# Block-recurrent cross attention with a maxout layer: state and A transposes moved from TensorE to DMA, a new prologue order, state reads in pairs

## The chip, the cores and the metric

The kernel runs on one core of one Trainium2 chip. The metric is the device time of one launch in microseconds (us). TensorE (PE) does the matmuls and the transposes through an identity matrix; VectorE (DVE) and ScalarE (ACT) move results out of the accumulation banks in PSUM and do elementwise work; GpSimd (POOL) does casts and products in SBUF; SyncE (SP) issues nearly all DMAs, in the order of the program. Each engine takes its own instructions in order and waits for the others by semaphores, so an instruction that waits holds up all behind it on its engine.

## What is computed

```python
B, H, S, Ns, D = 8, 8, 512, 32, 64
scale = 1 / sqrt(D)
a     = softmax(scale * x @ state^T)        # per batch and head, 512 x 32
xread = a @ state                           # 512 x 64
a2    = softmax(scale * state @ x^T)        # 32 x 512
sread = a2 @ x                              # 32 x 64
t     = concat([xread, sread], rows)        # 544 rows per batch; heads side by side: 4352 x 512
out   = max(t @ w1, t @ w2) @ w_out         # w1, w2: 512 x 1024, w_out: 1024 x 512
```

## The kernel before

**The algebra.** The maximum is rewritten: max(h1, h2) = h2 + relu(h1 - h2). With wd = w1 - w2 and wwo = w2 @ w_out, out = t @ wwo + relu(t @ wd) @ w_out. For the x rows, t is itself a product A @ state (A: the normalised weights), so the kernel first multiplies the states with the weights (SW = state x [wd, wwo], `sw_mm`, L301) and then A with SW. Per batch b: `xt` (x transposed), `sc` (scores, L214) and their exponential e on ACT, `red` (row sums and reciprocals, DVE), `nm` (the product a = e / sum, L240), `at` (a transposed into aT), `sw`, then `l1` (L334: r = relu(aT x SW), eight tiles f) and `l2` (L362: four output tiles c, each of two matmuls with aT and eight with r). `sr` (L270 to L293) is the second read: e^T x, scaled by its reciprocal sums (`sr_ev`, L280), transposed and put into sread_t, from which the last 256 output rows are made at the end (`m1`, `m2`).

**The states.** sbd (L105) holds, per batch and pair of heads, the transposed states of the two heads in block-diagonal form: for a pair k, partitions 0 to 63 carry head 2k in columns 0 to 31, and partitions 64 to 127 carry head 2k+1 in columns 32 to 63; the rest is zero. Before, sbd is set to zero as a whole (L440), `cS` (L160) casts the states to bf16 with each head written twice side by side (sb), `S` (L165) transposes 128x128 blocks on TensorE, and two evictions `S.lo.hi.j` (L173) copy only the diagonal parts. Steps S.0.1 and S.1.2 serve batches 0 and 1, S.2.4 and S.4.8 the batches 2 to 7. `sc` and `sw` read sbd.

**Transposes by DMA.** `xtd` (L200) makes xt of a batch from a bf16 copy of x (xb, written by `cb`), and `atd` (L256) makes aT from a. Batches 2 to 7 have both by DMA. Batches 0 and 1 have x and A transposed on TensorE (`xt`, `at`) and evicted by DVE or ACT.

**What sets the order.** The prologue, all work up to `sc`, `nm` and `atd` of batch 2, is one list written out, ORDER (L18 to L41), run token by token by `step` (L508). A token with `:` and bank numbers is TensorE work into those PSUM banks; a token with `>A`, `>V` or `>P` is work of ACT, DVE or POOL; a token with neither is a DMA, all on SP. The numbers are batch and part: `sw.0.3:1,4` is the fourth quarter of SW of batch 0 into banks 1 and 4, `sw.0.3.0>A` its first eviction by ACT, and `swh.1.0` is half a row of SW of batch 1. `ww.i.f0.f1` is part of wwo, `sub.q` part of wd = w1 - w2, `cw2` and `w2` cast, transpose and evict w2, `cwo` casts w_out. `l2p.0.c.f0.f1` is part of output tile c of batch 0, `l2o` its two matmuls with aT; `ld...` are loads. `idle.n.w` is n matmuls of w columns on a zero tile, which compute nothing. The order within each engine is the order of the list, so a bank that is not evicted yet or an eviction that stands behind a waiting one stops what follows.

Behind the list stands a loop over b = 1 to 6 (L526). An iteration issues the transposes for later batches, does `l1` of batch b, `sc`, `nm` and `atd` of batch n = b + 1, output tiles 0 and 1 of b, `sw` of n, the state reads of the batches in `rd` (L555) into one bank of ring "a" (two banks), then output tiles 2 and 3 of b and the store. Before, rd is (2, 0) and (3, 1) in the first two iterations and one batch in each of the other four.

Of the kernel before, what the change touches and what calls it, by code (L numbers as in the profile page):

```python
# [703 lines left out]
```

## Time and profile before

| | |
|---|---|
| three runs | 150.48, 151.10, 151.94 us; median 151.1 |
| the profiled execution | 151.55 us, its span 149.6 us |
| HBM read, written | 15.20 MB, 8.91 MB |
| granted TensorE clock | 1.00 |

The span is the part of the execution that the profile covers. A row of the timeline gives start (us from the span's start), length, engine, source line, operation, written tile <- read tiles, shape, count, and in brackets the idle time ahead of it with what ended it. A row of grouped instructions gives count, busy time and mean ns. In a windows row stand the stretch and its length, then busy time (and count) of PE, PEld (TensorE's weight loads), DVE, ACT and POOL, then the granted clock, the DMA share and GB/s. A DMA row gives count, size and time from issue to landing. "PEq" and "SPq" mean the engine's queue of issuing instructions. Matmuls are pipelined, so the distance between starts, not the length of a row, is what one costs.

### The profile page before, as it was taken

To read this page: it belongs to the slowest core of one execution; us is meant where nothing else is said; L and a number is where in the kernel's file an instruction comes from. 1 tells how busy PE (TensorE), PEld (TensorE's weight loads), DVE (VectorE), ACT (ScalarE), POOL (GpSimd) and SP (SyncE) were. 2 spreads that over 40 slices of the span, in tenths; PEclk is the share of its full clock that TensorE was granted. 3 is DMA by queue.
4 is the path that set the end of the run, shared out by engine and by line. 5 is a ranking of instruction groups with operands and counts; after the bars stand their busy time and mean duration, and the time that the engine had idled before them with its cause. 6 is when DMAs were issued, how large, how long until landed. Compare 5 with 4: busy or idle time off the path is not lost. (4 is left out here: it accounts for less than half of the span.)

```text
span 149.6 us, 3181 instructions
## 1 busy us (share of the span) xinstructions
PE 141.8 (95%) x1281; PEld 71.0 (47%) x1281; DVE 85.0 (57%) x167; ACT 65.9 (44%) x129; POOL 50.7 (34%) x71
## 2 busy tenths in 40 slices
PE   6979779999999999999999999999999999999991
PEld 2656334635445445444544454444445444763460
DVE  3599387976534917662848385558627575720320
ACT  5234544665594438163814554173528054520200
POOL 3123223389300960770582159045600500000000
PEclk9999999999999999999999999999999999999999
DMA  4999999953936199898879767997406031500423
GB/s 115 291 365 364 363 349 361 345 119 42 252 134 278 30 119 286 345 179 251 346 142 205 266 214 145 182 363 163 86 1 280 2 74 70 212 9 9 185 96 140
DMA packets 36692, 29.09 MB, mean 194 GB/s; under 512 B 21568, under 2 KB 34112, under 8 KB 35776
## 3 DMA queue, kind: packets, MB, share of 16 engines
q1 hardware_dynamic: 36400, 28.77, 67.4%
q8 instruction: 11, 0.18, 0.5%
q10 hardware_dynamic: 272, 0.07, 0.2%
q14 instruction: 9, 0.07, 0.2%
HBM read 15.20 MB, written 8.91 MB: 161 GB/s over the span
## 5 line engine op out<-in xcount | busy, mean ns | idle before, releaser
L354 PE MATMUL bank<-wo,r 128*128 128x512 bf16 (+1 forms) x264 | 62.0, 373 | 0.1
L354 PEld LDWEIGHTS <-r 128*128 128x128 bf16 x264 | 25.4, 98 | 29.3 <-issue 1.3
L95 ACT COPY h<-bank 128x512 f32<-128x512 f32 (+1 forms) x17 | 9.5, 574 | 48.0 <-PE bank L354 44.4
L339 PE MATMUL bank<-aT,sw 128*128 128x512 bf16 x128 | 30.1, 379 | 0.0
L330 DVE TENSOR_SCALAR r<-bank 128x512 bf16<-128x512 f32 x28 | 19.4, 692 | 17.5 <-PE bank L339 16.9
L328 ACT ACTIVATE r<-bank 128x512 bf16<-128x512 f32 x36 | 21.3, 612 | 7.3 <-PE bank L339 7.0
L97 DVE CAST sw<-bank 128x512 bf16<-128x512 f32 (+1 forms) x25 | 15.1, 653 | 11.5 <-PE bank L309 11.5
L241 POOL TENSOR_TENSOR a<-e,er 128x512 bf16<-128x512 bf16 x13 | 13.4, 1048 | 23.6 <-ACT e L233 13.7
L99 POOL CAST xb<-h 128x1024 bf16<-128x1024 f32 x12 | 12.2, 1039 | 22.4 <-issue 15.4
L349 PE MATMUL bank<-sw,aT 128*128 128x512 bf16 (+1 forms) x66 | 18.9, 373 | 0.2 <-ACT sr L287 0.2
L339 PEld LDWEIGHTS <-sw 128*128 128x128 bf16 x128 | 12.0, 98 | 12.9
L99 POOL CAST xe<-h 128x512 bf16<-128x512 f32 x27 | 15.8, 621 | 5.9 <-DMA h<-in_x_dram 5.2
L97 DVE COPY h<-bank 128x512 f32<-128x512 f32 (+1 forms) x16 | 10.5, 659 | 11.9 <-PE bank L354 9.9
L95 ACT CAST sw<-bank 128x512 bf16<-128x512 f32 (+1 forms) x27 | 13.2, 559 | 7.6 <-PE bank L309 7.6
L237 DVE TENSOR_REDUCE sums<-e 128x16 f32<-128x512 bf16 x16 | 10.6, 662 | 1.1 <-ACT e L233 1.0
L233 ACT ACTIVATE e<-bank 128x512 bf16<-128x512 f32 x16 | 8.9, 595 | 4.6 <-PE bank L225 4.1
L433 PE MATMUL bank<-wz 128*128 128x256 bf16 (+1 forms) x38 | 7.7, 349 | 1.2 <-DVE ones L438 1.2
L426 PE MATMUL bank<-wo,w2t 128*128 128x512 bf16 x32 | 8.1, 380 | 0.6 <-DVE w2t L97 0.6
L349 PEld LDWEIGHTS <-aT 128*128 128x128 bf16 x66 | 5.5, 98 | 4.8 <-issue 0.7
L309 PE MATMUL bank<-wd,sbd 64*32 64x512 bf16 (+1 forms) x144 | 5.9, 358 | 1.1 <-DVE wd L418 1.1
L99 POOL CAST wo<-h 128x1024 bf16<-128x1024 f32 x3 | 3.1, 1039 | 8.7 <-DMA h<-in_moe_w_out_dram 8.7
L225 PEld LDWEIGHTS <-xt 128*128 128x128 bf16 x128 | 5.0, 98 | 2.1 <-ACT xt L95 0.3
(71 smaller groups left out, 112.1 us busy)
## 6 DMA issues: line engine op xcount, KB each, us to landing
out_dram<-h SPq DMA_DIRECT2D x7, 1024.0 KB, 4.0
h<-in_moe_w_dram SPq DMA_DIRECT2D x8, 512.0 KB, 9.9
h<-in_x_dram SPq DMA_DIRECT2D x8, 512.0 KB, 7.3
h<-in_x_dram SPq DMA_DIRECT2D x3, 1024.0 KB, 6.5
h<-in_moe_w_out_dram SPq DMA_DIRECT2D x4, 512.0 KB, 9.3
h<-in_x_dram SPq DMA_DIRECT2D x4, 256.0 KB, 3.9
out_dram<-h SPq DMA_DIRECT2D x3, 256.0 KB, 2.4
out_dram<-rs SPq DMA_DIRECT2D x2, 256.0 KB, 2.4
```

Of the source, the lines that this page charges most:

```text
L95: nc.scalar.copy(o, i)
L97: nc.vector.tensor_copy(o, i)
L99: nc.gpsimd.tensor_copy(o, i)
L233: nc.scalar.activation(out=e_view(b, hh).rearrange("p (g c) i n -> p g c (i n)", g=2), in_=p.rearrange("p (c g m) -> p g c m", c=NC, g=2), ...
L237: nc.vector.tensor_reduce(es_all[:, b, hh], e_view(b, hh), axis=AXX, op=ALU.add)
L241: (nc.gpsimd if eng == "P" else nc.vector).tensor_mul(e_view(b, hh, "a"), e_view(b, hh), d_(b)["er"][:, hh].unsqueeze(3).to_broadcast([128 ...
L328: nc.scalar.activation(out=o, in_=p, func=ACTF.Relu)
L330: nc.vector.tensor_scalar(o, p, scalar1=0.0, scalar2=None, op0=ALU.max)
L339: nc.tensor.matmul(p, SW[b][:, g, f * 128:(f + 1) * 128], AT[b][:, g].rearrange("p c t -> p (c t)"), start=(g == 0), stop=(g == 1))
L349: nc.tensor.matmul(p[:, lo:hi], AT[b][:, g, c, :], SW[b][:, g, FF + lo:FF + hi], start=(start and g == 0), stop=(stop and g == 1))
L354: nc.tensor.matmul(p[:, lo:hi], R[b][:, f, c * 128:(c + 1) * 128], wo[:, f, lo:hi], start=(start and j == 0), stop=(stop and j == len(fs) ...
L426: nc.tensor.matmul(p, w2t[:, f, i, :], wo[:, f, :], start=(f == 0), stop=(f == NF - 1))
```

## The change

- The states of batches 2 to 7 no longer pass TensorE. A new step `cSm` (`s_mask`) on ACT multiplies the f32 states by one of two columns of a new constant tile zm (1 for the heads of one parity, 0 for the others), so that the zeros of the block-diagonal form stand in sb already. A new DMA, `std` (`s_dma`), transposes all twelve blocks from sb straight into sbd. Steps S.2.4, S.4.8, their evictions and cS.2.8 on POOL go. sbd is set to zero for batches 0 and 1 alone.
- A of batch 1 is transposed by DMA (`atd.1`); at.1.0, at.1.1 and their evictions go.
- On SP the order becomes: the states of batches 2 to 7 (ldS.2.8) ahead of x of batch 2, then atd.1, xtd.2, std, x of batch 3.
- ORDER is new as a whole: other engines for many evictions and casts, other banks, another order on TensorE, 44 instead of 34 fillers of 256 columns (and the same four of 512).
- State reads come as (0, 1), (2, 3), (4, 5), (6, 7) in iterations 1, 2, 4 and 6; iterations 3 and 5 have none.

```diff
--- before.py
+++ after.py
@@ -17,27 +17,26 @@
 
 ORDER = """
 ldS.0.1 ldxk.0.0 ldxk.0.1 ldxk.0.2 ldxk.0.3 ldw2.0.256 ldwo.0.2 ldw1.0.256 ldw2.256.512 ldwo.2.4 ldw1.256.512
-ldw2.512.768 ldwo.4.6 ldw1.512.768 ldx.1.0 ldx.1.1 ldw2.768.1024 ldwo.6.8 ldw1.768.1024 ldx.2.0 ldx.2.1 ldS.2.8
-idle.4.512:7 cS.0.1>A S.0.1:0 idle.7.256:2 S.0.1.0>V S.0.1.1>A ce.0.0>P cS.1.2>V xt.0.0:6 ce.0.1>V S.1.2:2
-S.1.2.0>A xt.0.0>V xt.0.1:3 idle.3.256:5 S.1.2.1>V xt.0.1>A ce.0.2>V ce.0.3>V xt.0.2:4 sc.0.0:5 xt.0.2>V xt.0.3:1
-sc.0.0>A idle.5.256:0 xt.0.3>V cw2.0>P red.0.0>V sc.0.1:7 idle.6.256:6 sc.0.1>A nm.0.0>V w2.0:0 cwo.0>A
-idle.8.256:2 w2.0>V red.0.1>V ww.3.0.2:6 sub.0.2.4>P ww.1.0.2:2 ww.0.0.2:3 ww.2.0.2:4 nm.0.1>V idle.5.256:1 cw2.1>A
-sub.0.0.2>V at.0.0:5 at.0.1:1 w2.1:7 at.0.0>V at.0.1>A cwo.1>P w2.1>V sw.0.0:0,5 sw.0.0.0>A sw.0.0.1>A ww.1.2.4:2
-sub.1.0.2>V l1.0.0:1 ww.2.2.4:4 sub.1.2.4>V l1.0.0>A ww.0.2.4:3 cw2.2>V sw.0.1:0,7 swh.1.0:5,1 sw.0.1.1>A
-ww.3.2.4:6 sw.0.1.0>V swh.1.0.0>A w2.2:7 swh.1.0.1>V l1.0.3:0 cwo.2>P w2.2>V l1.0.1:5 l1.0.3>A l1.0.2:1 l1.0.1>A
-ww.2.4.6:4 sub.2.0.2>V ww.3.4.6:6 l1.0.2>A ww.0.4.6:3 sub.2.2.4>V l2p.0.2.0.2:7 ce.1.0>V sw.0.2:0,5 l2p.0.2.2.4:7
-sw.0.2.1>A sw.0.2.0>V ce.1.1>P xt.1.0:1 l1.0.5:5 xt.1.0>V xt.1.1:0 ce.1.2>P l1.0.5>A l1.0.4:1 xt.1.1>V ww.1.4.6:2
-ce.1.3>A l1.0.4>V sc.1.0:5 l2p.0.0.0.2:0 sc.1.0>A cw2.3>V xt.1.3:1 l2p.0.2.4.6:7 xt.1.3>A red.1.0>V w2.3:5 xt.1.2:1
-l2p.0.0.2.4:0 cwo.3>P w2.3>V xt.1.2>A l2p.0.0.4.6:0 sc.1.1:1 nm.1.0>V ww.2.6.8:4 sc.1.1>A ww.1.6.8:2 sub.3.2.4>V
-ww.2>A ww.3.6.8:6 ww.0.6.8:3 red.1.1>V sub.3.0.2>P ww.1>A l2p.0.1.0.2:5 ww.3>A l2p.0.1.2.4:5 ww.0>V l2p.0.1.4.6:5
-nm.1.1>P sw.0.3:1,4 swh.1.2:2,6 sw.0.3.0>A sw.0.3.1>V l2p.0.3.0.2:3 cb.2.1>P swh.1.2.1>A swh.1.2.0>V at.1.0:1
-l1.0.6:4 at.1.0>A at.1.1:6 cb.2.0>P l1.0.7:2 l1.0.6>A at.1.1>V l2p.0.3.2.4:3 l1.0.7>V l1.1.2:1 ce.2.1>P xtd.2
-ldx.3.0 ldx.3.1 l1.1.3:6 l1.1.2>A ce.2.0>P l2p.0.2.6.8:7 l1.1.3>V ce.2.2>P l1.1.1:4 l2p.0.3.4.6:3 cS.2.8>P l1.1.1>A
-l2p.0.3.6.8:3 sw.0.4:2,1 swh.1.1:6,4 sw.0.4.1>A sw.0.4.0>V l2p.0.1.6.8:5 ce.2.3>P l2p.0.0.6.8:0 swh.1.1.0>A
-swh.1.1.1>V S.4.8:1 l2o.0.2:7 S.4.8.0>V l1.1.6:2 l2.0.2>A S.4.8.1>V l1.1.7:6 l1.1.6>A l1.1.5:4 l1.1.7>V l1.1.4:1
-l1.1.5>A l1.1.0:7 l1.1.4>A l2o.0.0:0 l2o.0.1:5 l1.1.0>A S.2.4:2 l2o.0.3:3 l2.0.1>A S.2.4.0>V l2.1.0:6 S.2.4.1>V
-l2.0.0>A l2.0.3>A store.0 sc.2.0:4 l2.1.0>V sc.2.1:1 sc.2.0>A l2.1.1:7 sc.2.1>A red.2.0>V red.2.1>V nm.2.0>P
-l2.1.1>V nm.2.1>P atd.2
+ldw2.512.768 ldwo.4.6 ldw1.512.768 ldx.1.0 ldx.1.1 ldw2.768.1024 ldwo.6.8 ldw1.768.1024 ldS.2.8 ldx.2.0 ldx.2.1
+idle.4.512:7 cS.0.1>V S.0.1:0 cS.1.2>A idle.1.256:2 S.0.1.0>V S.0.1.1>V S.1.2:1 idle.5.256:6 S.1.2.0>A S.1.2.1>A
+ce.0.0>V xt.0.0:2 idle.6.256:7 xt.0.0>A ce.0.1>A ce.0.2>A xt.0.1:6 idle.1.256:5 ce.0.3>V xt.0.1>A xt.0.2:7 xt.0.3:5
+xt.0.2>A sc.0.0:3 xt.0.3>V sc.0.0>A sc.0.1:4 idle.6.256:1 cw2.0>V sc.0.1>A red.0.0>V w2.0:0 idle.10.256:2 w2.0>A
+cwo.0>V red.0.1>V nm.0.0>P ww.1.0.2:1 ww.2.0.2:2 sub.0.2.4>V ww.3.0.2:6 ww.0.0.2:7 sub.0.0.2>V idle.4.256:4 cw2.1>A
+nm.0.1>P sw.0.0:5,3 idle.5.256:0 sw.0.0.1>V sw.0.0.0>V w2.1:4 cwo.1>V at.0.0:0 w2.1>A at.0.1:3 idle.6.256:5
+at.0.0>V at.0.1>A ww.1.2.4:1 sub.1.0.2>V ww.3.2.4:6 sub.1.2.4>V l1.0.0:5 l1.0.1:0 l1.0.0>V sw.0.1:4,3 l1.0.1>A
+ww.0.2.4:7 cw2.2>V ww.2.2.4:2 sw.0.1.1>A sw.0.1.0>A swh.1.0:5,0 w2.2:3 swh.1.0.1>A l2p.0.0.0.2:4 cwo.2>P w2.2>V
+swh.1.0.0>A l1.0.3:0 l1.0.2:5 l1.0.3>A ww.3.4.6:6 sub.2.2.4>V l1.0.2>A ww.0.4.6:7 ww.2.4.6:2 sub.2.0.2>V ww.1.4.6:1
+ce.1.0>V sw.0.2:3,0 l2p.0.0.2.4:4 sw.0.2.1>A sw.0.2.0>V ce.1.1>P xt.1.0:5 l1.0.4:0 xt.1.0>V xt.1.1:3 ce.1.2>P
+l1.0.4>A l1.0.5:5 xt.1.1>V ce.1.3>P xt.1.2:0 l1.0.5>A sc.1.0:3 xt.1.2>V sc.1.0>A xt.1.3:5 cw2.3>V l2p.0.0.4.6:4
+xt.1.3>A l2p.0.3.0.2:0 red.1.0>V w2.3:3 sc.1.1:5 cwo.3>A w2.3>V l2p.0.3.2.4:0 nm.1.0>P l2p.0.3.4.6:0 sc.1.1>A
+ww.1.6.8:1 sub.3.2.4>V ww.0.6.8:7 ww.1>A ww.2.6.8:2 sub.3.0.2>P ww.0>V l2p.0.2.0.2:3 ww.2>A l2p.0.2.2.4:3 red.1.1>V
+cSm.1>A l2p.0.2.4.6:3 sw.0.3:5,1 nm.1.1>P swh.1.1:7,2 sw.0.3.1>V sw.0.3.0>A ww.3.6.8:6 cSm.0>A swh.1.1.0>V l1.0.7:5
+cb.2.0>P atd.1 l1.0.6:1 swh.1.1.1>V ww.3>A l2p.0.1.0.2:7 l1.0.6>V l2p.0.1.2.4:7 cb.2.1>P l1.0.7>A l2p.0.1.4.6:7
+sw.0.4:2,6 ce.2.2>P xtd.2 swh.1.2:1,5 sw.0.4.0>A l2p.0.1.6.8:7 swh.1.2.0>V ce.2.3>P l2p.0.2.6.8:3 swh.1.2.1>A
+l2p.0.3.6.8:0 ce.2.0>P sw.0.4.1>A l1.1.4:2 ce.2.1>P l1.1.0:1 l1.1.4>A l1.1.3:5 l1.1.0>A l2o.0.2:3 l1.1.3>V l1.1.6:6
+l1.1.1:2 l2.0.2>V l1.1.6>A l1.1.2:1 std ldx.3.0 ldx.3.1 l1.1.1>A l2o.0.1:7 l1.1.2>V l1.1.5:5 l1.1.7:3 l2.0.1>V
+l1.1.5>A l2p.0.0.6.8:4 l1.1.7>A l2o.0.0:4 l2o.0.3:0 l2.0.0>V l2.1.0:6 l2.0.3>V store.0 sc.2.0:2 l2.1.0>A sc.2.1:1
+l2.1.1:7 sc.2.1>A sc.2.0>A red.2.1>V red.2.0>V nm.2.1>P l2.1.1>A nm.2.0>P atd.2
 """
 
 
@@ -100,6 +99,7 @@
 
 
     ident = consts.tile([128, 128], BF16, name="ident")
+    zm = consts.tile([128, 2], F32, name="zm")
     ones = consts.tile([128, 2], BF16, name="ones")
     wz = consts.tile([128, 512], BF16, name="wz")
     sbd = consts.tile([128, B, 4, 2 * Ns], BF16, name="sbd")
@@ -162,6 +162,17 @@
         copy(eng, sb[:, lo:hi].rearrange("p b g z d -> p (b g) z d"),
              sf[:, lo:hi].rearrange("p b g d -> p (b g) d").unsqueeze(2).to_broadcast([128, n, 2, D]))
 
+    def s_mask(z, eng):
+        o, i, m = sb[:, 2:B, :, z], sf[:, 2:B], zm[:, z:z + 1]
+        if eng == "A":
+            nc.scalar.activation(out=o, in_=i, func=ACTF.Copy, scale=m)
+        else:
+            (nc.vector if eng == "V" else nc.gpsimd).tensor_scalar(o, i, scalar1=m, scalar2=None, op0=ALU.mult)
+
+    def s_dma():
+        nc.sync.dma_start_transpose(out=sbd[:, 2:B].rearrange("p b (g k) t -> p (b g) (k t)", g=2),
+                                    in_=sb[:, 2:B].rearrange("p b g z d -> p (b g z d)"))
+
     def s_mm(lo, hi, ring="r"):
         p = bank(ring, BF16)
         for b in range(lo, hi):
@@ -437,8 +448,11 @@
     nc.vector.memset(wz, 0.0)
     nc.vector.memset(ones, 1.0)
     nc.scalar.activation(out=ones[:, 1:2], in_=ones[:, 0:1], func=ACTF.Exp)
-    nc.vector.memset(sbd, 0.0)
+    nc.vector.memset(sbd[:, 0:2], 0.0)
     make_identity(nc, ident)
+    nc.gpsimd.memset(zm, 0.0)
+    for i in range(4):
+        nc.gpsimd.memset(zm[32 * i:32 * i + 32, i % 2:i % 2 + 1], 1.0)
     for t in xe:
         for o in (7, 136):
             nc.gpsimd.memset(t.rearrange("p c k w -> p (c k) w")[:, :, o:o + 1], 1.0)
@@ -490,7 +504,7 @@
 
     mms = dict(S=mm_S, xt=mm_xt, sc=mm_sc, at=mm_at, w2=mm_w2, sw=mm_sw, swh=mm_swh, l1=mm_l1, ww=mm_ww, l2p=mm_l2p,
                l2o=mm_l2o, l2=mm_l2, idle=idle)
-    evs = dict(cS=s_cast, ce=cast_e, cb=cast_b, nm=nmul, cw2=w2_cast, sub=w_sub, cwo=wo_cast,
+    evs = dict(cS=s_cast, cSm=s_mask, ce=cast_e, cb=cast_b, nm=nmul, cw2=w2_cast, sub=w_sub, cwo=wo_cast,
                S=lambda lo, hi, j, eng: s_ev(ps["S", lo], lo, hi, j, eng),
                xt=lambda b, k, eng: xt_ev(ps["xt", b, k], b, k, eng),
                sc=lambda b, hh, eng: sc_ev(ps["sc", b, hh], b, hh),
@@ -503,7 +517,7 @@
                ww=lambda i, eng: ww_ev(ps["ww", i], i, eng),
                l2=lambda b, c, eng: l2_out(b, c, ps["l2", b, c], eng))
     dma = dict(ldS=load_s, ldx=load_x, ldxk=load_xk, ldw2=lambda lo, hi: load_w(2, moe_w2, lo, hi),
-               ldw1=lambda lo, hi: load_w(1, moe_w1, lo, hi), ldwo=load_wo, xtd=xt_dma, atd=at_dma, store=store)
+               ldw1=lambda lo, hi: load_w(1, moe_w1, lo, hi), ldwo=load_wo, xtd=xt_dma, std=s_dma, atd=at_dma, store=store)
 
     def step(tok):
         name, _, eng = tok.partition(">")
@@ -552,8 +566,8 @@
             l2(b, 0)
             l2(b, 1)
         pg = [sw_mm(n, 512 * z, 512 * z + 512) for z in range(3)]
-        rd = (n, b - 1) if b < 3 else (n,)
-        p = bank("a")
+        rd = (0, 1) if b == 1 else (b, n) if b % 2 == 0 else ()
+        p = bank("a") if rd else None
         for j, v in enumerate(rd):
             sr_mm(v, p, j)
         for z in range(3):
```

## The prediction

> **What bounds the kernel.** I read the page first, then the windows (busy time by stretch), then TensorE's timeline around the places that the change touches, then the DMA landings.
>
> ```profile
> PE 141.8 (95%) x1281; PEld 71.0 (47%) x1281; DVE 85.0 (57%) x167; ACT 65.9 (44%) x129; POOL 50.7 (34%) x71
> PE   6979779999999999999999999999999999999991
> PEclk9999999999999999999999999999999999999999
> ```
> ```profile
> 15.00:20.00 5.00, 3.27 (x41) 1.57 (x40) 2.34 (x5) 1.85 (x5) 1.04 (x1) 1.00 1.09 359
> 20.00:25.00 5.00, 5.00 (x47) 2.21 (x36) 4.18 (x8) 2.76 (x6) 1.75 (x2) 1.00 1.10 355
> ```
>
> TensorE is full from 20 us on at full clock; its holes lie before that, while DMA moves 355 to 359 GB/s. So I see two regimes: up to 20 us arriving weights set the pace, and from there each microsecond taken off TensorE comes off the end, if nothing new stalls it. A busy digit does not prove full speed, so I check the pitch in these timeline rows, three iterations of the loop over batches:
>
> ```profile
> 51.00 1.89 PE L354 MATMUL bank<-wo,r 128*128 128x512 bf16 x8
> 53.09 0.59 PE L349 MATMUL bank<-sw,aT 128*128 128x512 bf16 x2 [0.20 <-ACT sr L287]
> 65.52 1.89 PE L354 MATMUL bank<-wo,r 128*128 128x512 bf16 x8
> 67.38 0.59 PE L349 MATMUL bank<-sw,aT 128*128 128x512 bf16 x2
> 93.40 1.89 PE L354 MATMUL bank<-wo,r 128*128 128x512 bf16 x8
> 95.13 0.59 PE L349 MATMUL bank<-sw,aT 128*128 128x512 bf16 x2
> ```
>
> Eight matmuls of 512 columns take 95.13 - 93.40 = 1.73 us, 0.216 each: no slack. After the two-batch state reads (first two pairs) the same eight take 2.09 and 1.86: holes of 0.36 and 0.13 us, where the last output tile waits for the bank that ScalarE still reads (L287).
>
> The Trainium skill, "Perfetto Trace Analysis", section "Identifying the Most-Contended Engine", says that matmul occupancy is a poor measure and weight-load busy share a better one. By its measure (47% here) TensorE would be far from its limit, and removing work from it would gain nothing; the pitch above says otherwise, and I give that reading only the last rival below.
>
> **Part 1: 20 transposes leave TensorE.** These are S.4.8, S.2.4 (L170) and at.1.0, at.1.1 (L263). Their cost is the distance to the next start:
>
> ```profile
> 33.88 0.39 PE L263 MATMUL bank<-ident,a 128*128 128x128 bf16 x4
> 34.10 0.59 PE L339 MATMUL bank<-aT,sw 128*128 128x512 bf16 x2
> 34.53 0.39 PE L263 MATMUL bank<-ident,a 128*128 128x128 bf16 x4
> 34.76 0.59 PE L339 MATMUL bank<-aT,sw 128*128 128x512 bf16 x2
> 39.73 0.61 PE L170 MATMUL bank<-ident,sb 128*128 128x128 bf16 x8
> 40.18 0.59 PE L349 MATMUL bank<-sw,aT 128*128 128x512 bf16 x2
> 43.63 0.39 PE L170 MATMUL bank<-ident,sb 128*128 128x128 bf16 x4
> 43.86 1.03 PE L349 MATMUL bank<-sw,aT 128*128 128x512 bf16 x4
> ```
>
> 0.22 + 0.23 + 0.45 + 0.23 = 1.13 us, all in the full stretch: -1.13. Their six evictions (four on DVE for S, one each on ACT and DVE for A) and one POOL cast go too; I cost them at nothing, because DVE is busy 57% of the span and ACT 44%.
>
> **Part 2: the new prologue up to 20 us.** What ends the starved stretch now:
>
> ```profile
> 18.47 1.29 DVE L418 TENSOR_TENSOR wd<-h,h 128x512 bf16<-128x512 f32 x2 [2.04 <-DMA h<-in_moe_w_dram]
> 19.81 0.51 PE L309 MATMUL bank<-wd,sbd 64*32 64x256 bf16 x12 [0.31 <-DVE wd L418]
> ```
>
> The second quarter of w1 lands at 18.4, two subtractions end at 19.76, sw.0.1 runs. The loads up to the last of w1 keep their order, and the subtractions stay on DVE. I counted what TensorE has done ahead of sw.0.1: before, three `ww` and one `l1`; after, two `ww` and two `l1`: eight matmuls either way, same xt, sc, at, w2. So the full stretch starts at 19.8 with the same work left: 0. The ten extra filler matmuls lie ahead of that, in waits for weights. The other prologue moves (casts and normalisation between DVE, ACT and POOL, the smaller memset, five tiny POOL memsets) end before w1 does: 0. One thing can move that landing: an instruction fetch runs among the loads (DMA view, 14.5 to 16.5 us):
>
> ```profile
> q8 instruction: 1, 0.02, 3.6%
> ```
>
> 3.6% of 16 engines over 2 us is 1.15 us on one engine; an engine so delayed may be what makes w1 late. I expect a fetch at about the same place, and keep the other case as a rival.
>
> **Part 3: 20 to 32.6 us.** I replayed the new token order with durations of rows. TensorE has work nearly everywhere; three short waits appear.
>
> ```profile
> 19.95 0.69 DVE L97 CAST w2b<-h 128x1024 bf16<-128x1024 f32 x1 [0.19 <-DMA h<-in_moe_w_dram]
> 26.55 0.69 DVE L330 TENSOR_SCALAR r<-bank 128x512 bf16<-128x512 f32 x1
> 34.78 0.60 ACT L328 ACTIVATE r<-bank 128x512 bf16<-128x512 f32 x1
> ```
>
> cw2.2 now stands behind l1.0.0 on DVE: 19.76 + 0.69 + 0.69 = 21.14. TensorE wants it after the rest of sw.0.1, two `ww` and swh.1.0, 19.81 + 0.1 + 0.86 + 0.3 = 21.07: 0.07. l1.0.4 and l1.0.5 both go to ACT, with xt.1.2 and xt.1.3 behind them in the same banks. An `l1` started at 34.10 was evicted at 35.38, 1.28 later; TensorE is back at the bank after an `l1`, four transposes and an `l1`, 0.43 + 0.23 + 0.43 = 1.09 (transposes as in Part 1): 0.19. The second frees at 1.28 + 0.60 = 1.88, wanted four transposes and eight score matmuls later, 1.28 + 0.23 + 0.23 = 1.74: 0.14. Sum +0.40; bounds 0 and twice that.
>
> **Part 4: masks on ACT, head of line.** ACT's order becomes ww.2, cSm.1, sw.0.3.0, cSm.0, ww.3, l1.0.7. No row shows cSm; the nearest are two ACT casts:
>
> ```profile
> L95 ACT CAST w2b<-h 128x1024 bf16<-128x1024 f32 x1 | 1.0, 1045 | 1.9 <-DMA h<-in_moe_w_dram 1.9
> L95 ACT CAST sb<-sf 128x256 bf16<-128x256 f32 x1 | 0.4, 405 | 0.1
> ```
>
> For 768 columns 0.405 + 0.64 x 512/768 = 0.83 us each. The question is when the states land. Issues, and below them landing times of the last w1 quarter, the first half of x of batch 2, and the states:
>
> ```profile
> 21.59 0.71 SPq L148 DMA_DIRECT2D h<-in_moe_w_dram  x1
> 22.34 2.88 SPq L141 DMA_DIRECT2D h<-in_x_dram  x2
> 25.27 1.42 SPq L156 DMA_DIRECT2D sf<-in_state_dram  x1
> ```
> ```profile
> h<-in_moe_w_dram SPq DMA_DIRECT2D x1, 512.0 KB, 8.5
> ```
> ```profile
> h<-in_x_dram SPq DMA_DIRECT2D x1, 512.0 KB, 9.3
> ```
> ```profile
> sf<-in_state_dram SPq DMA_DIRECT2D x1, 384.0 KB, 8.9
> ```
>
> Landings: 30.1, 31.6, 34.2. Half of x takes 1.5, so the states take 34.2 - 31.6 - 1.5 = 1.1. Moved ahead of x they land at 30.1 + 1.1 = 31.2 (estimate); the other end is 34.2. TensorE:
>
> ```profile
> 32.98 0.30 PE L309 MATMUL bank<-wd,sbd 64*32 64x256 bf16 x8
> ```
>
> sw.0.3 started at 32.98; one `ww` (0.43) now stands behind it, so 32.6. Behind it come swh.1.1 and ww.3.6.8; l1.0.7 wants its evictions at 33.5. ACT needs 0.83 + 0.41 first (sw.0.3.0 is as wide as the second row), so states landed by 32.3 cost nothing. At 31.2: 0. Later ones cost one for one.
>
> **Part 5: A of batch 1 by DMA.** It waits for nm.1.1 on POOL.
>
> ```profile
> 31.80 0.69 DVE L97 CAST wwo<-bank 128x512 bf16<-128x512 f32 x1
> 31.94 1.04 POOL L241 TENSOR_TENSOR a<-e,er 128x512 bf16<-128x512 bf16 x1
> DMA to landing us min/median/max: 3.1/4.7/5.1
> ```
>
> DVE does ww.0 (0.69) ahead of red.1.1 now, so nm.1.1 ends not at 32.98 but at about 33.6. Landing is 3.1 to 5.1 us behind the issue (six aT transposes): 36.7 to 38.7. It is wanted by l1.1.4: behind 32.6 stand sw.0.3 and swh.1.1 (0.5), ww, l1.0.7, l1.0.6 (1.3), six `l2p` matmuls (1.3), sw.0.4 and swh.1.2 (0.65), six more (1.3): 37.65. DMA is all but empty at that time, so I take 3.1 and cost it at 0. Bounds 0 and 1.05.
>
> **Part 6: the states' transpose and SP's queue.** On SP stand atd.1, xtd.2, std, ldx.3, store.0.
>
> ```profile
> 35.12 2.44 SPq L202 DMA_TRANSPOSE xt<-xb  x1
> DMA to landing us min/median/max: 4.2/4.5/6.0
> ```
> ```profile
> 46.45 0.63 PE L225 MATMUL bank<-sbd,xt 128*128 128x64 bf16 x16
> ```
>
> cb.2.0 and cb.2.1 follow nm.1.1 on POOL, (casts as long as nm), so xtd.2 issues at 33.6 + 2 x 1.04 = 35.7 and holds SP to 38.1. std (12 blocks, between xt's 16 and aT's 8) lands by 38.1 + 6.0 = 44.1 at worst. sc.2.0, the third row, wants it at 46.45 - 1.13 = 45.3: 0, with 1.2 us to spare. ldx.3 leaves some 2 us later and serves a cast that stands behind nm.2 on POOL, so behind sc.2.0: 0.
>
> The Trainium skill, "VectorE: DVE Perf Modes", section "The three transpose paths", prices one 128x128 block at 390 ns on TensorE and 1309 ns by DMA, and its rule is to use TensorE where PSUM will do. Were blocks serial at that price, A's eight would land at 44 and stall TensorE 6.5 us; the landing rows (16 blocks in 4.5 us) speak against it.
>
> **Part 7: state reads in pairs.** 32 matmuls per batch as before, moved whole. Iterations 1 and 2 already read two batches; 4 and 6 now do, 3 and 5 read none. One read showed no hole (93.40 to 95.13), two showed 0.13 or 0.36: +0.26 (bounds 0 and 0.72).
>
> **Sum.** -1.13 + 0.40 + 0.26 = -0.47 us against the profiled execution's 151.55 us (span 149.6), giving 151.08. That execution stood 0.45 over the median of 151.1, so 150.6.
>
> **Rivals.**
> - *ACT stuck on the states (slower).* They land at 34.2 as now; cSm.1 holds sw.0.3.0 until 35.4, l1.0.7 starts 1.95 late: 150.6 + 1.95 = 152.55, more if the load's last packets trail further. It decides from a landing of 32.3 on. For: the last load trailed here. Against: the states are no longer last.
> - *A's transpose late.* Landing 4.7 behind the issue: 0.65 of stall, 151.25.
> - *The weights come earlier (faster).* If the fetch misses the engine that carries w1's second quarter, it lands one half megabyte's time, 1.5 us (Part 4), earlier at 16.9; the subtractions end at 18.2 and TensorE, by my replay, is ready for sw.0.1 at 18.5, 1.3 us earlier: 149.3. For: the new order changes instruction counts. Against: only by twenty or so.
> - *TensorE's time is not the bound*, so that the removal is worth nothing: 151.1 + 0.3 = 151.4. Against: the pitch.
>
> **Numbers.** Forecast 0.40 (150.6); states late 0.22; A late 0.08; weights earlier 0.24; removal worth nothing 0.06. A measurement of this kernel tells about 1% (1.5 us) from no change: the three runs span 150.48 to 151.94. The states' rival lies at the 1% edge and passes it with any trailing, so I count it as slower; weights earlier counts as faster, the rest as same: 0.24, 0.54, 0.22. Forecast alone: 149.9 to 151.5 (the bounds of Parts 3 and 7). For 8 in 10 the range takes in most of both outer cases: 149.4 to 152.6.
>
> **What would show it.** Right: no L170 rows behind 10 us and no L263 rows behind 20; sw.0.1 near 19.8, sw.0.3 near 32.6, l1.1.4 near 37.7, sc.2.0 near 45.5. Wrong: an idle ACT waiting for sf ahead of cSm.1, TensorE waiting for aT at l1.1.4 or for sbd at sc.2.0, or a full stretch that starts well off 19.8.

## The result, and the profile after

| | before | after |
|---|---|---|
| median of the runs made side by side (22 each) | 150.51 us | 151.80 us |
| lowest to highest | 149.69 to 152.29 | 150.57 to 153.68 |
| ratio, with its 95% interval | | 1.0075 [1.0051, 1.0098] |
| profiled execution, its span | 151.55, 149.6 us | 151.85, 150.1 us |

The changed kernel is slower by 0.75%, about 1.1 us; the forecast was faster by 0.5 us, within 1%. The size lies inside the bound of what I called no change, but the interval excludes 1, and the sign is the other one. The ratios, here and below, leave out executions in a second, slower state (three of after's 22), which the medians include.

One thing must be seen before the two profiles are laid side by side. The profiled execution of before was 1.04 us over the median of its kernel, that of after is at its own median. In both, TensorE's last matmul starts at 146.2 (146.23 and 146.16); the spans, 149.6 and 150.1, differ by what comes behind it, which the sum at the end takes up. The rest of the loss can't be found in that pair alone.

From the page after, the first table (busy time, share, instructions) and TensorE's row of tenths:

```profile
PE 141.8 (94%) x1252; PEld 71.2 (47%) x1271; DVE 80.4 (54%) x157; ACT 70.1 (47%) x136; POOL 48.9 (33%) x74
PE   6989989999999999999999999999999999999990
```

DVE lost 4.6 us and ACT gained 4.2: the masks and casts went where the change said. The windows of after, in the two stretches shown of before:

```profile
15.00:20.00 5.00, 4.54 (x43) 2.75 (x42) 3.39 (x7) 2.15 (x4) 0.00 (x0) 1.00 1.08 359
20.00:25.00 5.00, 5.00 (x42) 2.20 (x42) 3.17 (x6) 2.76 (x6) 1.88 (x2) 1.00 1.09 355
```

TensorE is now busy for 4.54 us of the stretch from 15 to 20, where before it was 3.27. That is filler, and it tells nothing of progress: see the timeline of TensorE after (start, length, line, tiles, count; L444 is the filler, L420 `w2.1`, L274 `at`, L437 `ww`, L350 `l1`, L320 `sw`).

```profile
14.74 0.72 PE L444 MATMUL bank<-wz 128*128 128x256 bf16 x5
15.30 0.61 PE L420 MATMUL bank<-ident,w2b 128*128 128x128 bf16 x8
15.75 0.61 PE L274 MATMUL bank<-ident,a 128*128 128x128 bf16 x8
16.20 0.82 PE L444 MATMUL bank<-wz 128*128 128x256 bf16 x6
17.02 1.04 PE L437 MATMUL bank<-wo,w2t 128*128 128x512 bf16 x4
17.89 1.03 PE L350 MATMUL bank<-aT,sw 128*128 128x512 bf16 x3
19.01 0.29 PE L320 MATMUL bank<-wd,sbd 64*32 64x256 bf16 x4
19.61 0.29 PE L320 MATMUL bank<-wd,sbd 64*32 64x256 bf16 x4 [0.31 <-DVE wd L429]
...
32.95 0.52 PE L320 MATMUL bank<-wd,sbd 64*32 64x256 bf16 x16
...
37.96 1.46 PE L350 MATMUL bank<-aT,sw 128*128 128x512 bf16 x6
...
45.73 0.63 PE L236 MATMUL bank<-sbd,xt 128*128 128x64 bf16 x16
```

In this execution sw.0.1 waits for the subtractions (its second half starts at 19.61, where before's profile had 19.81), as the prediction said it would. sw.0.3 at 32.95, l1.1.4 at 37.96, sc.2.0 at 45.73: each within 0.4 us of the prediction (32.6, 37.65, 45.5).

The DMA view of single issues shows what made before's profile an untypical one. In the window from 7.2 to 8.0 us the second quarter of w1 is the only load of w1 or w2 that is issued; columns: count, size, us from issue to landing. First before, then before_pairs, the kernel before with one line of the loop changed (below), which does the same up to there:

```profile
h<-in_moe_w_dram SPq DMA_DIRECT2D x1, 512.0 KB, 11.0
```
```profile
h<-in_moe_w_dram SPq DMA_DIRECT2D x1, 512.0 KB, 8.9
```

Issued at 7.33 and 7.62, it landed at 18.4 and at 16.5. Over all fourteen profiled executions of this study:

| kernels made from | landing of w1's second quarter (us) | us behind its first quarter, in the same order |
|---|---|---|
| before | 18.37 (before itself), 16.49, 16.47, 16.03, 16.72, 17.39, 16.13 | 4.42, 2.85, 2.86, 2.84, 2.86, 2.86, 2.86 |
| after | 18.18 (after itself), 16.63, 17.41, 17.73, 16.81, 17.10, 17.81 | 4.38, 2.86, 2.85, 4.50, 2.85, 2.86, 2.87 |

The landing differs by more than 2 us from one execution to the next, and two things move it. All loads together come earlier or later (the first quarter landed between 13.19 and 14.94), which moves the work ahead of the second quarter too. And in three of the fourteen, before itself and after itself among them, 1.5 us more pass between the two quarters. The prediction rested on that rarer case. I call the eleven others early. What happens when w1 lands early is the first question for the experiments.

### The profile page after: what moved, and what is told of

Same layout as the page of the kernel before. It is cut to its first block, busy times and chain, and to the rows that moved or that the text cites. A ratio compares the mean times of both kernels' runs of the same rounds, so it can differ in the third digit from the quotient of the medians.

```text
span 150.1 us, 3139 instructions
## 1 busy us (share of the span) xinstructions
PE 141.8 (94%) x1252; PEld 71.2 (47%) x1271; DVE 80.4 (54%) x157; ACT 70.1 (47%) x136; POOL 48.9 (33%) x74
## 5 line engine op out<-in xcount | busy, mean ns | idle before, releaser
L365 PE MATMUL bank<-wo,r 128*128 128x512 bf16 (+1 forms) x257 | 60.6, 372 | 1.0 <-issue 0.3
L94 ACT COPY h<-bank 128x512 f32<-128x512 f32 (+1 forms) x15 | 8.6, 572 | 47.7 <-PE bank L365 44.2
L350 PE MATMUL bank<-aT,sw 128*128 128x512 bf16 x127 | 29.9, 379 | 0.3 <-DMA aT<-a 0.3
L252 POOL TENSOR_TENSOR a<-e,er 128x512 bf16<-128x512 bf16 x16 | 17.1, 1084 | 35.1 <-DVE er L249 22.1
L350 PEld LDWEIGHTS <-sw 128*128 128x128 bf16 x128 | 12.3, 98 | 14.1 <-issue 0.4
L96 DVE COPY h<-bank 128x512 f32<-128x512 f32 (+1 forms) x18 | 11.7, 657 | 12.1 <-PE bank L365 11.3
L360 PE MATMUL bank<-sw,aT 128*128 128x512 bf16 (+1 forms) x57 | 17.0, 372 | 0.2
L444 PE MATMUL bank<-wz 128*128 128x256 bf16 (+1 forms) x48 | 9.5, 339 | 1.2 <-DVE ones L449 1.2
L437 PE MATMUL bank<-wo,w2t 128*128 128x512 bf16 x31 | 7.9, 380 | 0.1
L429 DVE TENSOR_TENSOR wd<-h,h 128x512 bf16<-128x512 f32 x7 | 5.8, 859 | 1.7 <-DMA h<-in_moe_w_dram 1.6
L320 PE MATMUL bank<-wd,sbd 64*32 64x512 bf16 (+1 forms) x144 | 5.9, 358 | 0.7 <-DVE wd L429 0.6
L444 PEld LDWEIGHTS <-wz 128*128 128x128 bf16 x48 | 5.0, 113 | 2.8 <-DVE ones L449 1.2
```

Source lines behind the costliest of these rows:

```text
L94: nc.scalar.copy(o, i)
L96: nc.vector.tensor_copy(o, i)
L252: (nc.gpsimd if eng == "P" else nc.vector).tensor_mul(e_view(b, hh, "a"), e_view(b, hh), d_(b)["er"][:, hh].unsqueeze(3).to_broadcast([128 ...
L350: nc.tensor.matmul(p, SW[b][:, g, f * 128:(f + 1) * 128], AT[b][:, g].rearrange("p c t -> p (c t)"), start=(g == 0), stop=(g == 1))
L360: nc.tensor.matmul(p[:, lo:hi], AT[b][:, g, c, :], SW[b][:, g, FF + lo:FF + hi], start=(start and g == 0), stop=(stop and g == 1))
L365: nc.tensor.matmul(p[:, lo:hi], R[b][:, f, c * 128:(c + 1) * 128], wo[:, f, lo:hi], start=(start and j == 0), stop=(stop and j == len(fs) ...
```

## The experiments

Theory: when w1 lands early, the new head (everything ahead of sw.0.1) isn't ready for it; two fillers and an eviction on ACT put TensorE 0.85 us behind the old head, and behind the head the change saves about what was forecast. Rivals: the paired reads cost it; TensorE's time isn't the bound, so that the removal brings nothing; the loss lies in the loop, where x and A of batch 3 come late. All kernels were timed in five rounds; ratios are to the kernel before on the same chip.

**before_pairs**: the reads alone.

```diff
-        rd = (n, b - 1) if b < 3 else (n,)
-        p = bank("a")
+        rd = (0, 1) if b == 1 else (b, n) if b % 2 == 0 else ()
+        p = bank("a") if rd else None
```

> Kernel before with one edit: the state reads in pairs, (0, 1), (2, 3), (4, 5), (6, 7) in iterations 1, 2, 4, 6. Theory: pairing costs nothing worth measuring (a second read costs 0.31 us and a hole of 0.13, a single one 0.30 and 0.12 for the change of weights), so 0 +- 0.3 us. Rival: the pairs carry the loss of about 1 us, so +0.8 to +1.2 us, ratio near 1.007.

Measured 1.0009 [0.9970, 1.0048]; after_oldreads undoes the same line.

**after_oldreads**: after with the line as it was before (the diff above, reversed).

> Changed kernel with the state reads of before, (2, 0), (3, 1), then one per iteration. Theory: the loss stays, ratio to the kernel before 1.005 to 1.010. Rival (the pairs carry it): ratio 1.000 or less.

Measured 1.0049 [1.0008, 1.0090]. The pairs alone cost nothing that can be told, and without them the change is still slower: they are not the cause. The starts of `sw` from one iteration to the next say why they are neutral: 14.53, 14.28, 13.85, 13.85, 13.85 us before, 14.72, 14.70, 13.43, 14.29, 13.43 after. An iteration without a read is 0.42 shorter, one with two is 0.44 longer.

These two also make the pair of profiles that the first pair was not, since w1 landed at 16.49 in the one and 16.63 in the other. The timeline of before_pairs, TensorE and then DVE (L409 is `w2.1`, L426 `ww`, L309 `sw`, L97 the eviction, L418 the subtractions):

```profile
14.76 0.62 PE L409 MATMUL bank<-ident,w2b 128*128 128x128 bf16 x8
...
16.17 0.61 PE L426 MATMUL bank<-wo,w2t 128*128 128x512 bf16 x2 [0.55 <-DVE w2t L97]
...
18.00 0.52 PE L309 MATMUL bank<-wd,sbd 64*32 64x256 bf16 x16
```
```profile
15.42 0.69 DVE L97 COPY w2t<-bank 128x1024 bf16<-128x1024 bf16 x1 [0.46 <-PE bank L409]
16.59 1.29 DVE L418 TENSOR_TENSOR wd<-h,h 128x512 bf16<-128x512 f32 x2 [0.47 <-DMA h<-in_moe_w_dram]
```

And of after_oldreads, TensorE, ACT, DVE:

```profile
14.75 0.72 PE L444 MATMUL bank<-wz 128*128 128x256 bf16 x5
15.31 0.61 PE L420 MATMUL bank<-ident,w2b 128*128 128x128 bf16 x8
...
16.20 0.82 PE L444 MATMUL bank<-wz 128*128 128x256 bf16 x6
17.02 1.04 PE L437 MATMUL bank<-wo,w2t 128*128 128x512 bf16 x4
...
18.85 0.30 PE L320 MATMUL bank<-wd,sbd 64*32 64x256 bf16 x8
```
```profile
15.95 1.01 ACT L94 COPY w2t<-bank 128x1024 bf16<-128x1024 bf16 x1 [1.12 <-PE bank L420]
```
```profile
16.73 1.29 DVE L429 TENSOR_TENSOR wd<-h,h 128x512 bf16<-128x512 f32 x2
```

Read the two heads side by side. Old: w2.1 at 14.76, evicted by DVE 15.42 to 16.11, `ww.1.2.4` at 16.17, eight matmuls, sw.0.1 at 18.00, just behind the subtractions (17.88). New: five fillers stand ahead of w2.1, which starts 0.55 later at 15.31; ACT evicts it 15.95 to 16.96 (1.01 instead of 0.69); six more fillers run to 17.0; `ww.1.2.4` at 17.02; eight matmuls; sw.0.1 at 18.85. The subtractions were over at 18.02, so 0.83 us of that is TensorE's own lateness. Only where the second quarter of w1 lands 4.4 us behind the first do both heads wait for it alike, as in the two first profiles.

**before_nostates**: before without the states of batches 2 to 7.

```diff
-... ce.2.2>P l1.1.1:4 l2p.0.3.4.6:3 cS.2.8>P l1.1.1>A
+... ce.2.2>P l1.1.1:4 l2p.0.3.4.6:3 l1.1.1>A
-swh.1.1.1>V S.4.8:1 l2o.0.2:7 S.4.8.0>V l1.1.6:2 l2.0.2>A S.4.8.1>V ...
+swh.1.1.1>V l2o.0.2:7 l1.1.6:2 l2.0.2>A ...
-... l1.1.0>A S.2.4:2 l2o.0.3:3 l2.0.1>A S.2.4.0>V l2.1.0:6 S.2.4.1>V
+... l1.1.0>A l2o.0.3:3 l2.0.1>A l2.1.0:6
```

> Kernel before without the cast, the transposes and the evictions of the states of batches 2 to 7 (their sbd stays zero, so the outputs of these batches are others). TensorE has 0.68 us less to do ahead of the loop, and nothing is put on DMA for it. Theory: the loop takes it back, because l1 of batch 3 waits for its A, whose landing (69.4 in both traces) hangs on loads and POOL and not on TensorE; before it had only 0.28 us to spare there. So -0.3 us at most, ratio 0.998 to 1.000. Rival (TensorE bounds throughout): -0.68 us, ratio 0.9955.

Measured 0.9957 [0.9926, 0.9988]: 0.65 us (interval 0.2 to 1.1), for transposes priced at 0.68 in the prediction. My expectation, 0.998 to 1.000, is reached by the upper edge of the interval alone; the measured value is that of its rival, that TensorE bounds throughout. The timeline agrees: from sw.0.3 to sc.2.0 it takes 12.80 us (31.56 to 44.36), before_pairs 13.46. Removing TensorE work here is worth about its full price, so the prediction's rival "TensorE's time is not the bound" falls. The prediction weighed against its own reading the Trainium skill, "Perfetto Trace Analysis", section "Identifying the Most-Contended Engine", by which the weight loads' 47% would leave room; in this kernel the pitch was the better measure, and this run decides between them.

**after_nmfirst**: in the loop, the casts and the transpose of x of batch b + 2 are moved behind the product and the transpose of A of batch n.

```diff
-            if b + 2 < B:
-                for g in range(2):
-                    cast_b(b + 2, g, "P")
-                xt_dma(b + 2)
 ...
+            if b + 2 < B:
+                for g in range(2):
+                    cast_b(b + 2, g, "P")
+                xt_dma(b + 2)
```

> Changed kernel; in iterations 2 to 5 the casts and the DMA transpose of x of batch b + 2 stand behind the normalisation and the A transpose of batch b + 1, on POOL and on SP. Theory: A of batch 3 then lands about 66 instead of 69.5, the wait of 0.4 us at l1 of batch 3 goes, and the time falls by 0.4 us or more: ratio to the kernel before 1.000 to 1.005. Rival (the loss lies elsewhere): ratio stays 1.0075.

Measured 1.0021 [0.9989, 1.0053], where after has 1.0075: about 0.8 us back, though the intervals touch. From sc.2.0 to the start of l1 of batch 3 the timelines give 0.40 of it (23.81 us in after, 45.77 to 69.18 here). What it takes away is seen in after on TensorE, SP and POOL:

```profile
58.28 0.64 PE L236 MATMUL bank<-sbd,xt 128*128 128x64 bf16 x16 [0.26 <-DMA xt<-xb]
...
69.54 2.75 PE L350 MATMUL bank<-aT,sw 128*128 128x512 bf16 x12 [0.25 <-DMA aT<-a]
```
```profile
62.53 1.78 SPq L213 DMA_TRANSPOSE xt<-xb  x1
64.55 1.75 SPq L268 DMA_TRANSPOSE aT<-a  x1
```
```profile
61.46 1.04 POOL L98 CAST xb<-h 128x1024 bf16<-128x1024 f32 x1 [0.79 <-DMA h<-in_x_dram]
62.46 2.06 POOL L252 TENSOR_TENSOR a<-e,er 128x512 bf16<-128x512 bf16 x2
```

POOL waits for x of batch 4 before it casts it, the product for A of batch 3 stands behind that cast, and A's transpose stands on SP and in the DMA engines behind x's. It lands at 69.50, 4.9 us behind its issue, and l1 of batch 3 starts there. With the loop changed, A's transpose goes first; SP's rows and TensorE's `l1` in after_nmfirst:

```profile
62.74 1.25 SPq L268 DMA_TRANSPOSE aT<-a  x1
64.70 1.32 SPq L213 DMA_TRANSPOSE xt<-xb  x1
```
```profile
69.18 3.19 PE L350 MATMUL bank<-aT,sw 128*128 128x512 bf16 x14
```

A landed at 65.78, 3.0 us behind its issue, and l1 no longer waits for it. So this place sets a date of its own: whatever TensorE saves earlier, it may not start l1 of batch 3 before x of batch 4 has come in.

**before_slowhead**: before with the two delays of the new head put in, a filler ahead of w2.1 and its eviction on ACT.

```diff
-sub.0.0.2>V at.0.0:5 at.0.1:1 w2.1:7 at.0.0>V at.0.1>A cwo.1>P w2.1>V ...
+sub.0.0.2>V at.0.0:5 at.0.1:1 idle.5.256:7 w2.1:7 at.0.0>V at.0.1>A cwo.1>P w2.1>A ...
```

> Kernel before with two steps of its head made like the changed kernel's: five filler matmuls of 256 columns ahead of w2.1, and w2.1 evicted by ACT (1.01 us) instead of DVE (0.69). Theory: that is where the change loses; where the second quarter of w1 lands near 16.5, sw.0.1 starts at about 18.9 instead of 18.0 and the whole kernel is 0.7 to 0.9 us longer, where it lands near 18.3 nothing is lost. On the mean of executions +0.4 to +0.9 us, ratio 1.003 to 1.006. Rival (the head is hidden behind the loads, as the prediction had it): 1.000.

Measured 1.0032 [0.9995, 1.0069]: in the direction of the theory, 0.5 us, with 1 barely inside. Its timeline of TensorE shows the lateness itself:

```profile
17.06 0.61 PE L426 MATMUL bank<-wo,w2t 128*128 128x512 bf16 x2 [0.87 <-ACT w2t L95]
...
18.89 0.52 PE L309 MATMUL bank<-wd,sbd 64*32 64x256 bf16 x16
```

w1 landed at 16.72 here, and sw.0.1 started at 18.89 as in after_oldreads, not at 18.00.

**after_fasthead**: after with the head's three delays taken out: both fillers, and the eviction back on DVE, for which `cwo.1` leaves DVE.

```diff
-nm.0.1>P sw.0.0:5,3 idle.5.256:0 sw.0.0.1>V sw.0.0.0>V w2.1:4 cwo.1>V at.0.0:0 w2.1>A at.0.1:3 idle.6.256:5
+nm.0.1>P sw.0.0:5,3 sw.0.0.1>V sw.0.0.0>V w2.1:4 cwo.1>P at.0.0:0 w2.1>V at.0.1:3
```

> Changed kernel with the head step undone: no filler between sw.0.0 and ww.1.2.4, w2.1 evicted by DVE, cwo.1 cast by POOL. Theory: ww.1.2.4 starts at 16.4 instead of 17.0, sw.0.1 at 18.2 instead of 18.85 where w1 lands early; 0.4 to 0.7 us less than the changed kernel's 1.0075: ratio 1.003 to 1.005. Rival (loss lies in the DMA moves): 1.0075.

Measured 0.9987 [0.9960, 1.0014], against 1.0075 [1.0051, 1.0098] for after: the intervals are apart, and one line of the order takes the whole loss away. `ww.1.2.4` now waits for the copy alone:

```profile
16.77 1.04 PE L437 MATMUL bank<-wo,w2t 128*128 128x512 bf16 x4 [0.34 <-DVE w2t L96]
...
18.60 0.30 PE L320 MATMUL bank<-wd,sbd 64*32 64x256 bf16 x8
```

**after_nofiller** and **after_evictv**: one of the three alone. The first takes out `idle.5.256:0` only, the second moves `w2.1` to V and `cwo.1` to P and keeps both fillers (the diff above, in parts).

> Changed kernel without the five filler matmuls between sw.0.0 and w2.1, nothing else. Theory (the filler holds w2.1 back until 15.3 though its cast is done at 14.85): w2.1 0.45 us earlier, and with it ww.1.2.4 at 16.55 instead of 17.0; 0.3 to 0.6 us of the 1.3 us that the whole head step gave: ratio 1.003 to 1.006. Rival (only the eviction engine counts): 1.0075.

> Changed kernel with w2.1 evicted by DVE and cwo.1 cast by POOL, all fillers kept. Theory: ww.1.2.4 waits for the eviction at 16.6 instead of 16.96, but the six fillers ahead of it end at 16.8 in any case: 0.1 to 0.3 us, ratio 1.005 to 1.007. Rival (the engine alone gave the 1.3 us): 0.999.

Measured 1.0049 [1.0010, 1.0089] and 1.0061 [1.0035, 1.0088]: each gives back less than its interval can tell. The timelines say how much each could. From sw.0.0, which waits for w1's first quarter, to `ww.1.2.4` pass 2.51 us in after (14.51 to 17.02), 2.10 in after_nofiller (13.98 to 16.08), 2.33 in after_evictv (14.69 to 17.02) and 1.80 in after_fasthead (14.97 to 16.77). So the delays stand in series: with the first filler gone the second ends last, and with the eviction on DVE the second filler still does. 0.41 and 0.18 us are 0.27% and 0.12%, where 0.26% and 0.14% were measured, closer than these intervals can warrant; for all three, 0.71 us or 0.47%, the measured 0.88% is more than the timeline shows.

All early executions together give the price of the head without the shift of the loads: from the landing of w1's first quarter to the start of sw.0.1.

| head | us, one for each early execution |
|---|---|
| old: before_pairs, before_nostates, before_nmfirst, before_dma, before_dma_nmfirst | 4.36 in all five |
| new: after_oldreads, after_nmfirst | 5.08, 5.08 |
| before_slowhead; after_evictv | 5.03; 4.88 |
| after_fasthead, after_fasthead_nmfirst | 4.36, 4.36 |

So the new head costs 0.72 us when w1 is early (the 0.85 of the pair above holds 0.13 by which all loads came later), and the edit of after_fasthead takes away all of it.

**before_dma**: the other half of the change alone. The old head and order up to sw.0.3, with the masks, `std`, `atd.1` and the load of the states from the new kernel, and a tail that I ordered by hand.

```diff
-... ldw2.768.1024 ldwo.6.8 ldw1.768.1024 ldx.2.0 ldx.2.1 ldS.2.8
+... ldw2.768.1024 ldwo.6.8 ldw1.768.1024 ldS.2.8 ldx.2.0 ldx.2.1
...
+nm.1.1>P sw.0.3:1,4 swh.1.2:2,6 sw.0.3.0>A sw.0.3.1>V l2p.0.3.0.2:3 cb.2.0>P atd.1 swh.1.2.1>A swh.1.2.0>V
+l1.0.6:4 cb.2.1>P l1.0.7:2 l1.0.6>A cSm.1>A l2p.0.3.2.4:3 l1.0.7>V ce.2.1>P xtd.2
+l2p.0.2.6.8:7 ce.2.0>P l2p.0.3.4.6:3 ce.2.2>P cSm.0>A std ldx.3.0 ldx.3.1
...
```

> The DMA moves alone: the order, fillers and state reads of the kernel before up to sw.0.3, then cSm on ACT, std, atd.1 as in the changed kernel, with l1 of batch 1 put behind the parts of l2 so that A has time to land. Theory (new head and short waits carry the loss, the moves are a gain): sc.2.0 comes 1.1 us earlier than before, of which the waits for x and A of batch 3 in the loop take back 0.3 to 0.8: ratio 0.995 to 0.998. Rival (the DMA transposes themselves cost): 1.003 or more, with TensorE waiting for aT at l1 of batch 1 or for sbd at sc.2.0.

Measured 1.0008 [0.9974, 1.0041]: a miss. No gain of the expected size is to be seen. All that TensorE gains (126.40 us from sw.0.1 to its last matmul's start, before_pairs 126.79) is lost again behind that matmul, where this kernel takes 0.49 us longer (see the sum, redone). From sw.0.3 to sc.2.0 its timeline takes 12.90 us (32.05 to 44.95) where before_pairs takes 13.46, so half of the 1.13 arrives; my tail has holes of its own (four `l1` take 1.02 us at 33.00, not 0.87, and eight `l2p` 2.13 at 34.02, not 1.73), and l1 of batch 3 waits for A again, landing 68.46, `l1` at 68.51.

**before_dma_nmfirst**: the same with the loop edit of after_nmfirst.

> The same, and in the loop the casts and the transpose of x of batch b + 2 behind the normalisation and the A transpose of batch b + 1. Theory: the wait for A of batch 3 goes, what is left is the wait for x of batch 3: 0.3 to 0.5 us less than the run before, ratio 0.991 to 0.995. Rival (TensorE never waits there in usual executions): same as the run before.

Measured 0.9971 [0.9938, 1.0003], above the expected span of 0.991 to 0.995. The sign is as expected, the size isn't, and the holes of the hand-made tail stay in it.

**before_nmfirst**: the loop edit on before.

> Kernel before with the loop edit alone. Theory: in executions with early weights TensorE waits 0.25 to 0.35 us for A of batch 3 in the kernel before too, so -0.2 to -0.4 us, ratio 0.997 to 0.999. Rival (the wait is new with the change): 1.000.

Measured 1.0011 [0.9982, 1.0040]. The expected gain isn't seen, though the interval doesn't exclude its lower end. The timeline has 0.26 us of it (from sc.2.0 to l1 of batch 3 23.19 us, before_pairs 23.45), but before itself, with its late w1, takes 23.19 without the edit. The date that it moves binds where TensorE arrives early.

**after_fasthead_nmfirst**: both edits on after.

> Changed kernel with the fast head (no filler between sw.0.0 and ww.1.2.4, w2.1 on DVE, cwo.1 on POOL) and, in the loop, the normalisation and A transpose of batch b + 1 ahead of the casts and x transpose of batch b + 2. Theory: both gains add, 0.9987 less the 0.3 to 0.8 us that the second edit gave: ratio 0.993 to 0.997, faster than both kernels. Rival (the two remove the same loss): 0.9987.

Measured 0.9931 [0.9904, 0.9959], median 149.94 us: faster than both kernels. The two repairs add up (0.88% and 0.54% alone, 1.44% together).

## Why the prediction was wrong, point by point

Two things failed: Part 2, which put the new head at 0 where it costs 0.72 us whenever w1 is early, and the end of the program, for which the prediction has no term and where the change costs 0.49. The waits that it puts into the loop are a smaller third.

**Part 2, "the full stretch starts at 19.8 with the same work left: 0", is the step that failed.** It took the landing of w1's second quarter in one execution, 18.4 us, for the kernel's. There the old head was waiting for w1 and the new one would be too. In eleven of the fourteen traces w1 lands early. The old head is ready for that; the new one isn't, and starts sw.0.1 0.72 us later. "The ten extra filler matmuls lie ahead of that, in waits for weights" names the cover, but not what it costs if the cover is gone: fillers hold w2.1 from 14.75 to 15.31 and `ww.1.2.4` to 17.02. And the move of the w2.1 eviction from DVE to ACT isn't named; it falls under "the other prologue moves", costed at 0 because they "end before w1 does". It took 1.01 instead of 0.69 on the chain that decides when w1 is early.

**The rival "the weights come earlier" had the right mechanism on the wrong kernel.** It priced an early landing (sw.0.1 at 18.5, gain 1.3 us) for the changed kernel, on the premise that an early landing would be new. It was the rule for the old one, sw.0.1 at 18.00 in before_pairs and at 17.55 in before_nmfirst, and the new head was ready at 18.85 and not at the 18.5 of the replay. The median of 22 runs, 150.51, already lay 1.04 under the profiled execution; with the three first runs (median 151.1) the gap was 0.45, and the prediction used it only to shift its sum. Such a gap says that the profiled execution is not typical and asks which wait in it could vary. An instruction fetch as the reason for the delay, which that rival assumed, was not settled: fetches run in that stretch in early and late executions alike. What makes w1 late stays open.

The rival "TensorE's time is not the bound" was priced at 151.4. With Parts 3 and 7 in full, 0.66 and not 0.3, it would have been 151.8, the measured median. That is chance: before_nostates rules this rival out.

**Part 1 (-1.13) was right.** before_nostates gives 0.65 for the 0.68 of the states. In after, sw.0.3 to sc.2.0 takes 12.78 us, before 13.47 (32.98 to 46.45): 0.69 less, although a `ww` of 0.43 was moved into that stretch: 1.12.

**Part 3 (+0.40) was right.** From sw.0.1 to sw.0.3 after_oldreads takes 13.35 us (18.85 to 32.20) and before_pairs 13.26 (18.00 to 31.26), the latter with that `ww` of 0.43 in it: +0.52. The dates of Parts 4 to 6 leave this term out: 32.98 less the `ww` is 32.55, and with +0.40 sw.0.3 is due at 32.95 and sc.2.0 at 45.7, which is what after shows (32.95, 45.73).

**Parts 4 to 6 were right in what they said.** Rows of after: the masks by tile on ACT; the two issues on SP; and landing behind issue (least, median, most) of aT and of sbd:

```profile
L168 ACT ACTIVATE sb<-sf,zm x2: 937/938/938, 32.2 to 33.6; 128x768 bf16<-128x768 f32 x2
```
```profile
34.13 1.35 SPq L268 DMA_TRANSPOSE aT<-a  x1
...
37.50 2.24 SPq L173 DMA_TRANSPOSE sbd<-sb  x1
```
```profile
DMA to landing us min/median/max: 3.0/3.1/4.9
```
```profile
DMA to landing us min/median/max: 6.3/6.3/6.3
```

The states landed at 31.33 (estimate 31.2) and no mask waited long; a mask took 0.94 us (estimate 0.83). A of batch 1 landed at 37.27 and was wanted at 37.96. `std` landed at 43.81 (bound 44.1) and was wanted at 45.73. The Trainium skill, "VectorE: DVE Perf Modes", section "The three transpose paths", has 1309 ns for a block by DMA; the eight blocks of A landed together 3.1 us behind the issue, so the serial reading that the prediction gave up was rightly given up. The 0 for ldx.3, which "leaves some 2 us later", looked only at batch 2. Nothing was said of what x of batch 3 and 4 and A of batch 3 do behind it, and there sc.3 and l1 of batch 3 each waited for a DMA (0.26 and 0.25 in the rows above). From sc.2.0 to l1 of batch 3 that made +0.29 to +0.62 us, the third row of the table below.

**Part 7 (+0.26) was too high** by the timelines: from l1 of batch 3 to the last matmul's start 76.62 us in before_pairs and 76.59 in before. The measured ratio alone couldn't tell 0.26 from nothing.

**The sum, redone.** The two pairs of profiles, cut into the same stretches (us; sw.0.1 is taken at its second half in the late pair, where it waits between the two):

| stretch | before_pairs, after_oldreads (w1 early) | before, after (w1 late) | forecast |
|---|---|---|---|
| start to sw.0.1 | 18.00, 18.85: +0.85 | 19.81, 19.61: -0.20 | 0 |
| sw.0.1 to sc.2.0 | 26.72, 26.13: -0.59 | 26.64, 26.12: -0.52 | -0.73 |
| sc.2.0 to l1 of batch 3 | 23.45, 23.74: +0.29 | 23.19, 23.81: +0.62 | 0, and +0.26 (Part 7) for it and the row below |
| l1 of batch 3 to the last matmul's start | 76.62, 76.58: -0.04 | 76.59, 76.62: +0.03 | |
| last matmul's start to the end of the span | 3.42, 3.91: +0.49 | 3.41, 3.91: +0.50 | no term |
| span | 148.21, 149.21: +1.00 | 149.64, 150.07: +0.43 | -0.47 |

The landing of w1 is chance in the first row: of the +0.85, 0.72 is the head, and the -0.20 is no gain of the change.

**The last row but one is a step that the prediction does not have.** Below are, for before and then after, the last copy out of PSUM, and what SP does from the landing of the last store (148.76 and 148.81):

```profile
146.53 0.37 ACT L95 COPY h<-bank 128x256 f32<-128x256 f32 x1 [4.19 <-PE bank L354]
```
```profile
L699 SPq EVENT_SEMAPHORE  x1: 28/28/28, 148.8 to 148.8; - x1
```
```profile
146.47 0.37 ACT L94 COPY h<-bank 128x256 f32<-128x256 f32 x1 [4.19 <-PE bank L365]
```
```profile
L713 SPq EVENT_SEMAPHORE  x7: 27/28/28, 148.8 to 149.2; - x7
```

At the end of the program SP waits for the DMAs' eight semaphores, one after the other in a fixed order. The trace names the semaphore of each DMA, and they go round in turn. With 56 DMAs the last store has the one that is waited for last; the two DMAs more, `std` and `atd.1`, give it the second of the eight, so that six further waits stand behind its landing: 0.37 us. The other 0.12 us is that the last store itself lands 1.94 to 1.95 us behind its issue instead of 1.83; why isn't known. All five kernels with 56 DMAs take 3.41 to 3.42 us for this stretch, and all nine with 58, before_dma with its old head among them, 3.90 to 3.91. No run changes the number of DMAs alone.

So when w1 is early the head costs 0.72, the end 0.49 and the waits in the loop 0.29, against the 0.59 saved: about 0.9 us of span, of which the times of two whole executions show some 0.1 less (151.00 against 150.12 for spans 1.00 apart). When w1 is late about 0.6 is left, without the chance in the first row. Measured were 1.1 us with an interval of 0.8 to 1.5. Summed the same way from sw.0.1 on, against before_pairs, after_fasthead comes to +0.13 us, before_dma to +0.10 and after_fasthead_nmfirst to -0.60, where -0.2, +0.1 and -1.0 were measured, each with 0.4 to 0.5 either way. That undoing the head's line brought 0.88% and not the 0.47% of its timeline stays open.

## What to carry to other kernels

A wait that ends with a DMA has no fixed length: before anything is hidden under it, ask how early that transfer can land and what the chain beside it would then cost, and treat a profiled execution that stands off its median as a sign that such a wait varies. Filler work on an in-order engine is not free idle time; put it behind the work whose input may arrive early, or make it short. And after a saving, look for the next date that a load or a transpose sets: here a loop order that cost nothing measurable in the old kernel took back part of what the new one gained. Last, compare the stretch behind the last matmul too: two DMAs more cost half a microsecond there, as much as the forecast gain, in both profiles from the start.
